# Two-stage attention and MoE kernel: who issues two early loads, who casts, and which pairs are transposed by TensorE

## The chip, the cores and the metric

One core of a Trainium2 chip. The metric is the device time of one execution, in microseconds (us). The kernel before takes 324.14 us, the median of 3 runs that lie between 324.01 and 324.51 us.

## The reference

What is computed, cut to its core (8 batches, 8 heads, 576 positions, head size 64; then 4608 tokens, 512 features, 2048 hidden):

```python
q_d, k_d, v_d = (mean over each 4 positions of q, k, v)
out_up    = repeat(softmax(q_d k_d^T / 8) v_d, 4)           # pooled attention
scores    = where(|i - j| < 4, q k^T / 8, -1e9)
out_local = softmax(scores) v                                # banded attention
x = (out_up + out_local) as [tokens, heads * head size]
h = x @ w_in
out = (h - tanh(h)) @ w_out
```

## The kernel before

**Pairs.** The attention works on pairs of heads, `p` = 0 to 31, four pairs (`j` = 0 to 3) to each batch `b`. What a pair makes is written, transposed, into `xT[j]`, 128 features by 576 tokens. The dense part takes a batch (512 tokens for an even one, 640 in pieces of 320 for an odd one): the first product L795 reads all four `xT[j]` of the batch, ScalarE takes tanh (L806), VectorE subtracts (L809, tile `gT`), and the second product L831 uses `gT` of the batch before; the result is copied (L846) and stored (L850).

**One pair, step by step.**
- Loads: q and k (`qkn`, L335) and v (`vst`, L368), all issued from SyncE's queue.
- Cast: `qkn` to bf16, reordered, in `qr`. Up to pair 15 these are two instructions at L521, one for each head of the pair, and each waits for both loads.
- Into feature-major form, tile `qk`: pairs 0 to 9 by nine TensorE transposes (L552) and a copy from PSUM (L556); pairs 10 to 31 by a DMA transpose (L526, tile `qT`) and two copies (L534). The list `TIN` says which.
- Pooling: `half` (L569) and `qkd` (L575 or L582).
- Scores: for pairs 0 to 3 a bias matrix is multiplied in first (L598, L607). Four of five blocks are s1 (L592), the fifth and the pooled scores are s2 (L592, L615). Up to pair 13 s1 and s2 stand apart in TensorE's order, from pair 14 they stand together (merged: the list `MERGE`, cut at `SPLIT`).
- Exponentials on ScalarE (L639 for s1, L652 and L655 for s2). A mask is multiplied in (L644, L660), or, from pair 12 on, a bias is added before the exponential (L634).
- Outputs: L669 (banded) and L675 (pooled) into PSUM; reciprocal and product on VectorE (L686, L688, tile `ln`).
- The way back: pairs 0 to 3 by twelve small products (L699, L702) and a copy (L767); pairs 4 to 7, 11 and 15 by TensorE transposes (L737, L738, L743), a copy of the pooled part (L762) and two adds (L754, L755); the rest by a DMA transpose (L705, tile `lT`) and two adds on GpSimd or VectorE (L717, L721). The list `XOUT` says which.
- v: a cast (L435, tile `vw`), pooled on TensorE (L449, L451, L471, L473) with a copy to `vd` (L454, L478) for the early pairs, by other means later.

**Order.** The instructions are first recorded as a list with costs and priorities; the class `Program` then simulates the engines, lets each pick what comes first by priority and dependence, picks an engine where a step has alternatives, and fixes the order on each engine's queue. So a change of a list or of a priority moves many instructions. The table `SHIFTS` adds to the priority of single steps, by their number, and can take an engine away from a step's choice. `P.shared` holds the steps that the planner takes to slow VectorE and GpSimd alike. Where the plan leaves TensorE idle before the dense part, filler matmuls (L1013) on a zeroed tile are put in; they use PSUM banks that are free.

**Limits on buffers around the change.** `qkn` has 4 buffers, `qr`, `qk`, `ln`, `lT`, `qT` and `E` have 2. From pair 12 on, the loads of a pair also wait in the plan until the DMA transpose L705 of the pair five before it has been issued (`GATE`, `BEHIND`).

Of the kernel before, what the change touches and what calls it, by code (L numbers as in the profile page):

```python
# [15 lines left out]
class Program:  # L16
# [21 lines left out]
    def op(self, eng, ns, fn, reads=(), writes=(), pri=0):  # L38
        i = len(self.ops)
        deps = set()  # L40
        for key in reads:
            if key in self.last_write:
                deps.add(self.last_write[key])
        for key in writes:
            if key in self.last_write:
                deps.add(self.last_write[key])
            deps.update(self.readers.get(key, ()))
        for key in reads:
            self.readers.setdefault(key, set()).add(i)
        for key in writes:  # L50
            self.last_write[key] = i
            self.readers[key] = set()
        deps.discard(i)
        if eng == "DMA":
            self.moves[i - 1] = i
        self.ops.append((eng, ns, fn, deps, pri))
        self.touch.append(set(reads) | set(writes))
        return i
# [93 lines left out]
    def emit(self, banks=None, end=None, filler=None):  # L152
        order = self.order()
        fill = {}
        if filler:
            until = min(self.start[i] for i in range(len(self.ops)) if end in self.touch[i])
            self.uses = {name: sorted(
                (self.start[i], self.start[i] + self.ops[i][1] + 200, i in self.fresh)
                for i in range(len(self.ops)) if self.touch[i] & set(keys))
                for name, keys in banks.items()}  # L160
            for i, name, room in self.idle(order, banks, until):
                if self.start[i] < 7000:
                    fill[i] = (name, int(min(8, room / 430) + max(0, 0.85 * room - 3440) / 220))
                else:
                    fill[i] = (name, int(0.8 * room / 220))
        for i in order:
            if i in fill:
                filler(*fill[i])
            if self.ops[i][2] is not None:
                self.ops[i][2]()  # L170
# [3 lines left out]
def kernel(  # L174
# [14 lines left out]
    NPAIR = B * NP  # L189
# [70 lines left out]
    P = Program()  # L260
# [66 lines left out]
    def load_qk(p):  # L327

        b, h0, s = p // NP, 2 * (p % NP), p % NQKN
        if LOAD[p] == 'row':  # L330
            for i, src in enumerate((q, k)):
                queue = nc.scalar if i and p < BYACT else nc.sync

# [151 lines left out]
    def attention(p):  # L485
# [16 lines left out]
        if LOAD[p] == 'tok':  # L502
            P.choice([(eng, ns, lambda fn=fn: fn(
                out=qr[s].rearrange("p a h d -> p (a h d)"),
                in_=qkn[sn].rearrange("p h c -> p (h c)"))) for eng, ns, fn in CAST_QK],
                     reads=[("qkn", sn, 0), ("qkn", sn, 1)],
                     writes=[("qr", s, 0), ("qr", s, 1)], pri=pri - 12)
            if TIN[p] == 'dma':
                op("SP", 1300, lambda: nc.sync.dma_start_transpose(
                    out=qk[s].rearrange("p i c -> p (i c)").rearrange(  # L510
                        "p (t c) -> p t c", c=128),
                    in_=qr[s].rearrange("p a h d -> p (a h d)")),
                   reads=[("qr", s, 0), ("qr", s, 1)],
                   writes=[("qk", s, 0), ("qk", s, 1), ("qTq", s)], pri=-50)
                op("DMA", 1300, None, reads=[("qTq", s), ("qr", s, 0), ("qr", s, 1)],
                   writes=[("qk", s, 0), ("qk", s, 1)], pri=pri)
        else:
            for hh in range(2):
                dst = qr[s][:, :, hh]
                srt = qkn[sn][:, hh].rearrange("p (a d) -> p a d", d=D)  # L520
                P.choice([(eng, ns, lambda dst=dst, srt=srt, fn=fn: fn(out=dst, in_=srt))  # L521
                          for eng, ns, fn in (any3[2:] if p >= CASTS else any3[:1] + any3[2:] if 0 < p < NOACT else any3)],
                         reads=[("qkn", sn, 0), ("qkn", sn, 1)],
                         writes=[("qr", s, hh)], pri=pri - 12)
        if TIN[p] == 'dma' and LOAD[p] == 'row':
            op("SP", 1300, lambda: nc.sync.dma_start_transpose(  # L526
# [5 lines left out]
            for i in range(2):  # L532
                def put(fn, i=i):
# [5 lines left out]
                         reads=[("qT", s)], writes=[("qk", s, i)], pri=pri)  # L539
        elif TIN[p] == 'pe':  # L540
            if p in APART:
# [153 lines left out]
        def back():  # L695
            for t, c, n in PIECES:
# [6 lines left out]
                         up[rows, t % 4, lead:lead + n], start=False, stop=True)  # L703
        if XOUT[p] == 'dma':
            op("SP", 1300, lambda: nc.sync.dma_start_transpose(  # L705
# [161 lines left out]


    EARLY, BIASED = 8, 4
    SPLIT = 14  # L870
    LOAD = ['row'] * NPAIR
    TIN = ['pe'] * 10 + ['dma'] * (NPAIR - 10)
    MERGE = [0] * EARLY + [2] * (SPLIT - EARLY) + [1] * (NPAIR - SPLIT)
    XOUT = ['pe' if p < 8 or p in (11, 15) else 'dma' for p in range(NPAIR)]
    PUT = [[("ACT", 535, A.copy), ("DVE", 620, V.tensor_copy)]] * 2
    W_PRI = [[5, 31, 32, 33], [-3, -2, -1, 0]]
    W_AT = (6, 6, 7, 7)
# [6 lines left out]
    V_ACT = ()  # L884
    FORE = 12
    GATE, BEHIND = range(12, NPAIR), 5
    BYACT = 0
    DIRECT, T_P = 16, 960
    T_IN, T_OUT = 1550, 1200
    NOACT = 0  # L890
# [1 line left out]
    HOLD = 2  # L892
    PADD = [p for p in range(NP, NPAIR) if XOUT[p] == 'pe']
    SOON = (0, 0, 0, 0)
# [68 lines left out]
    for p in range(2):  # L963
        prep_v(p)
    work = [attention(p) for p in range(NPAIR)]
    for a in work:
        next(a)
    next(work[0])
    for p in range(NPAIR):
# [23 lines left out]
    dense(B)  # L993

    SHIFTS = {
        70: (124, None), 80: (0, 'ACT'), 98: (211, None), 266: (212, None),
        325: (100, None), 388: (303, None), 643: (4864, None), 649: (0, 'DVE'),
        655: (50, None), 669: (50, None), 820: (62, None), 828: (-100, None),
        1248: (-105, None),
    }  # L1000
    for i, (shift, other) in SHIFTS.items():
        o = P.ops[i]
# [42 lines left out]
```

## Time and profile before

| | before |
|---|---|
| median of the runs | 324.14 us (324.01 to 324.51) |
| the profiled execution's own time | 324.28 us |
| its span, from the first to the last instruction | 322.5 us |
| TensorE matmul busy | 315.1 us, 98% of the span, 2661 instructions |
| VectorE, ScalarE, GpSimd busy | 216.5, 218.7, 194.1 us |
| granted TensorE clock, by the records | 1.00 |

The profile shows one execution. A line name such as L795 is a line of the kernel before; PE is TensorE's matmul, PEld its weight load, DVE VectorE, ACT ScalarE, POOL GpSimd, SP SyncE, which here only issues DMAs. In a timeline row stand the start in us, the length in us, the engine, line, operation, output and input, the shape, and how many instructions the row holds. Matmuls run into one another, so a row's length has some 0.15 us of a last matmul's tail in it: how long a stretch holds TensorE is read from one row's start to the next row's start. In brackets stand the idle time ahead of the row and what ended it.

### The profile page before, as it was taken

Reading aid. Unit: us, or ns where it says so; the run is one execution under the profiler, and the core shown is the slowest. Engines: PE = TensorE matmul, PEld = TensorE weight load, DVE = VectorE, ACT = ScalarE, POOL = GpSimd, SP = SyncE. Lnnn points to the kernel's source line nnn. Section 1 sums busy time; section 2 is a strip of 40 time slices with the busy share of each in tenths; the row PEclk is TensorE's granted clock in tenths of the full one; section 3 lists DMA queues with packets and bytes.
Section 4 is the critical chain, followed back from the end, with each engine's and each line's share of the span. In section 5 each row is a group of like instructions: output and inputs, shape, how many; then the busy total and the mean of one; then the engine's idle time right before and its main releaser. Section 6 shows DMA issues by size and latency. Waiting matters only on the chain.

```text
span 322.5 us, 7217 instructions
## 1 busy us (share of the span) xinstructions
PE 315.1 (98%) x2661; PEld 175.4 (54%) x2661; DVE 216.5 (67%) x397; ACT 218.7 (68%) x382; POOL 194.1 (60%) x271
## 2 busy tenths in 40 slices
PE   7889999999999999999999999999999999999996
PEld 3464545566654445666655445666654445566544
DVE  6778886887886577768667676766776454554312
ACT  2865997579997977699887769669975434555300
POOL 5578866468766789889999877997954100000000
PEclk9999999999999999999999999999999999999999
DMA  7999999699996899999999999998423211000012
GB/s 210 279 390 368 367 382 307 181 206 202 248 262 125 227 261 266 242 255 207 243 231 296 263 249 252 251 266 234 105 71 82 63 42 57 35 34 35 34 70 94
DMA packets 112832, 64.42 MB, mean 200 GB/s; under 512 B 90556, under 2 KB 96028, under 8 KB 112796
## 3 DMA queue, kind: packets, MB, share of 16 engines
q1 hardware_dynamic: 112796, 63.95, 77.4%
q8 instruction: 21, 0.34, 0.5%
q14 instruction: 15, 0.12, 0.1%
HBM read 42.96 MB, written 9.44 MB: 162 GB/s over the span
## 4 chain that ended last, share of the span: by engine, by line
PE 85%; DMA 6%; SPq 3%; POOL 2%; DVE 2%; issue 1%; ACT 0%; POOLq 0%
PE ps_hy L831 38%; PE ps_hy L795 36%; DMA gT<-in_moe_w_in_dram 3%; DMA qkn<-in_k_dram 3%; PE ps_ox L592 3%; PE ps_ox L669 3%; PE ps_ox L675 2%; SPq L335 2%; PE ps_ox L615 1%; SPq L368 1%; PE ps_ox L552 1%; DVE gT L809 1%; PE ps_ox L743 1%; POOL w_in_sb L428 1%; POOL E L660 1%
## 5 line engine op out<-in xcount | busy, mean ns | idle before, releaser
L795 PE MATMUL ps_hy<-xT,w_in_sb 128*128 128x320 bf16 (+1 forms) x768 | 147.9, 326 | 0.7 <-DVE gT L809 0.7
L831 PE MATMUL ps_hy<-w_out_sb,gT 128*128 128x512 bf16 (+2 forms) x608 | 144.4, 368 | 0.0
L809 DVE TENSOR_TENSOR gT<-ps_hy,u 128x320 bf16<-128x320 f32 (+1 forms) x192 | 103.4, 553 | 59.4 <-ACT u L806 57.5
L806 ACT ACTIVATE u<-ps_hy 128x320 f32<-128x320 f32 (+1 forms) x192 | 92.6, 496 | 55.8 <-PE ps_hy L795 50.2
L795 PEld LDWEIGHTS <-w_in_sb 128*128 128x128 bf16 x768 | 71.6, 98 | 52.4 <-issue 0.6
L831 PEld LDWEIGHTS <-gT 128*128 128x128 bf16 x608 | 56.5, 98 | 52.3
L569 POOL TENSOR_TENSOR half<-qk 128x576 f32<-128x576 bf16 x30 | 34.7, 1155 | 29.3 <-ACT qk L534 17.9
L534 ACT COPY qk<-qT 128x576 bf16<-128x576 bf16 x43 | 51.1, 1210 | 0.0
L688 DVE TENSOR_TENSOR ln<-ps_ox,r 128x896 bf16<-128x896 f32 x32 | 34.9, 1090 | 1.0
L521 POOL CAST qr<-qkn 128x576 bf16<-128x576 f32 x48 | 31.9, 677 | 4.6 <-DMA qkn<-in_k_dram 4.4
L639 ACT ACTIVATE E<-ps_ox 128x912 bf16<-128x912 f32 x28 | 26.2, 935 | 1.9 <-DVE ps_ox L634 1.2
L634 DVE TENSOR_TENSOR ps_ox<-ps_ox,bias 128x912 f32<-128x912 f32 x20 | 22.2, 1111 | 4.6 <-PE ps_ox L592 4.6
L846 DVE COPY y<-ps_hy 128x512 f32<-128x512 f32 (+2 forms) x22 | 14.1, 640 | 16.6 <-PE ps_hy L831 16.1
L435 POOL CAST vw<-vst 128x640 bf16<-128x640 f32 x31 | 23.6, 760 | 1.4 <-DMA vst<-in_v_dram 1.4
L660 POOL TENSOR_TENSOR E<-E,mask 128x240 bf16<-128x240 bf16 x23 | 15.2, 662 | 15.0 <-ACT E L652 14.7
L397 POOL TENSOR_TENSOR vp<-vp 72x512 f32<-72x512 f32 x16 | 20.3, 1268 | 0.0
L669 PEld LDWEIGHTS <-E 128*128 128x128 bf16 x320 | 16.3, 98 | 5.7
L669 PE MATMUL ps_ox<-vw,E 128*128 128x65 bf16 x320 | 19.4, 194 | 0.0
L655 ACT ACTIVATE E<-ps_ox 72x576 bf16<-72x576 f32 (+1 forms) x28 | 18.7, 668 | 0.0
L675 PE MATMUL ps_ox<-vd,E 128*128 128x65 bf16 (+1 forms) x256 | 18.2, 193 | 0.3 <-DVE vd L478 0.3
L592 PEld LDWEIGHTS <-qk 64*128 64x128 bf16 x320 | 9.1, 94 | 16.3 <-issue 12.5
L652 ACT ACTIVATE E<-ps_ox 128x240 bf16<-128x240 f32 x28 | 10.4, 370 | 7.4 <-PE ps_ox L615 6.2
(101 smaller groups left out, 264.6 us busy)
## 6 DMA issues: line engine op xcount, KB each, us to landing
vst<-in_v_dram SPq DMA_DIRECT2D x64, 160.0 KB, 4.3
qkn<-in_q_dram SPq DMA_DIRECT2D x32, 288.0 KB, 4.2
qkn<-in_k_dram SPq DMA_DIRECT2D x32, 288.0 KB, 4.3
out_dram<-y SPq DMA_DIRECT2D x35, 256.0 KB, 2.4
vp<-in_v_dram SPq DMA_DIRECT2D x15, 320.0 KB, 4.9
gT<-in_moe_w_in_dram SPq DMA_DIRECT2D x4, 1024.0 KB, 8.2
xT<-in_moe_w_out_dram SPq DMA_DIRECT2D x8, 256.0 KB, 4.6
gT<-in_moe_w_out_dram SPq DMA_DIRECT2D x2, 1024.0 KB, 8.7
```

Of the source, the lines that this page charges most:

```text
L435: P.choice([(eng, ns, lambda fn=fn: fn(out=vw[w][:, 2 * jj:2 * jj + 2, :, 0:64], in_=vst[s])) for eng, ns, fn in CAST_V[p >= NEARLY]], rea ...
L521: P.choice([(eng, ns, lambda dst=dst, srt=srt, fn=fn: fn(out=dst, in_=srt)) for eng, ns, fn in (any3[2:] if p >= CASTS else any3[:1] + any ...
L534: fn(out=full[:, i].rearrange("p (g a) -> p g a", a=A9), in_=qT[s][:, :, i::2].rearrange("p a g -> p g a"))
L569: eng.tensor_tensor(out=half, in0=four[:, :, :, 0:2], in1=four[:, :, :, 2:4], op=ALU.add)
L639: op("ACT", 820, lambda: A.activation(out=e1, in_=ps[:, :, 0:456], func=AF.Exp, scale=SCALE), reads=ts, writes=[("E", s, 0)], pri=pri)
L669: T.matmul(po[:, hh, 65 * t:65 * t + 65], E[s][:, c:c + 128], vw[w][:, 2 * jj + hh, t, :], start=True, stop=True)
L675: T.matmul(po[:, hh, o:o + 65], E[s][0:kp, c + gw * i:c + gw * i + 128], vd[w][0:kp, jj, 2 * hh + i, :] if direct else vd[w][:, i, 2 * jj ...
L688: op("DVE", 1010, lambda: V.tensor_tensor(out=ln[s].rearrange("p n (h d) -> p h n d", d=D), in0=blocks[:, :, :, 0:64], in1=r[s].unsqueeze( ...
L795: T.matmul(ps_hy[slot][:, 0:n], w_in_sb[:, dc, fc * 128:(fc + 1) * 128], xT[dc][:, t0 + c0:t0 + c0 + n], start=(dc == 0), stop=(dc == N_DC ...
L806: op("ACT", 90 + 76 * n // 100, lambda: A.activation(out=u[us][:, 0:n], in_=ps_hy[slot][:, 0:n], func=AF.Tanh), reads=[("hy", slot)], writ ...
L809: op("DVE", 70 + 105 * n // 100, lambda: V.tensor_tensor(out=gT[g][:, fc, c0:c0 + n], in0=ps_hy[slot][:, 0:n], in1=u[us][:, 0:n], op=ALU.s ...
L831: T.matmul(ps_hy[slot][:, 0:c1 - c0], gT[g][:, fc, ts * 128:ts * 128 + 128], w_out_sb[:, fc, c0:c1], start=(fc == 0), stop=(fc == N_FF - 1))
```

## The change

- The loads of k for pairs 0 and 1 are issued from ScalarE's queue (`BYACT` = 2).
- The casts L521 of q and k join the steps that the planner takes to be shared between VectorE and GpSimd, which makes it choose other engines.
- Pairs 10 and 11 come in through TensorE too (`TIN`), so in all pairs 0 to 11.
- Pairs 11 and 15 go back by DMA (`XOUT`), as their neighbours do.
- Merged scores from pair 12 on (`SPLIT`): pairs 12 and 13 are new in it.
- The number of fillers comes from another formula.
- The table of shifts is replaced as a whole, 22 entries for 13.

```diff
@@ Program.emit
-                if self.start[i] < 7000:
-                    fill[i] = (name, int(min(8, room / 430) + max(0, 0.85 * room - 3440) / 220))
-                else:
-                    fill[i] = (name, int(0.8 * room / 220))
+                slow = 430 if self.start[i] < 7000 else 220
+                fill[i] = (name, min(9, int(0.82 * room / slow)))
@@ the casts of q and k
+                P.shared.add(len(P.ops))
@@ the lists
-    SPLIT = 14
+    SPLIT = 12
-    TIN = ['pe'] * 10 + ['dma'] * (NPAIR - 10)
+    TIN = ['pe'] * 12 + ['dma'] * (NPAIR - 12)
-    XOUT = ['pe' if p < 8 or p in (11, 15) else 'dma' for p in range(NPAIR)]
+    XOUT = ['pe' if p < 8 else 'dma' for p in range(NPAIR)]
-    BYACT = 0
+    BYACT = 2
@@ the shifts, two of 13 and two of 22 entries
     SHIFTS = {
-        70: (124, None), 80: (0, 'ACT'),
...
+        73: (148, None), 75: (148, None),
...
```

The loads' queue is chosen by `queue = nc.scalar if i and p < BYACT else nc.sync` (L332, where `i` is 1 for k).

**What moves, place one: ScalarE at the start of the program.** Before, from the table load on (`qkn_72` and `qkn_73` hold q and k of pairs 0 and 1, `qr_87` is the cast for pair 0, `qr_88` for pair 1, `vd_84` the pooled v of pairs 0 and 1, `qk_89` is used by pairs 0 and 2, `qk_90` by pairs 1 and 3):

```order
L916 ACT_TABLE_LOAD
L916 CAST u_111<-lT_100 1x1
L556 COPY qk_89<-ps_ox 128x128x4
L521 CAST qr_88<-qkn_73 128x9x64
L639 ACTIVATE E_98<-ps_ts 128x912
L556 COPY qk_90<-ps_ox_118 128x128x4
L652 ACTIVATE E_98<-ps_ts 128x240
L655 ACTIVATE E_98<-ps_ts 128x640
L639 ACTIVATE E_99<-ps_ts_123 128x912
L556 COPY qk_89<-ps_ts 128x1152
L652 ACTIVATE E_99<-ps_ts_123 128x240
```

And in the changed kernel, whose line numbers are one or two lower:

```order
L333 DMA qkn_72<-in_k_dram 64x2x576
L333 DMA qkn_73<-in_k_dram 64x2x576
L915 ACT_TABLE_LOAD
L915 CAST u_111<-lT_100 1x1
L520 CAST qr_87<-qkn_72 128x9x64
L555 COPY qk_89<-ps_ox 128x128x4
L520 CAST qr_88<-qkn_73 128x9x64
L638 ACTIVATE E_98<-ps_ts 128x912
L555 COPY qk_90<-ps_ox_118 128x128x4
L651 ACTIVATE E_98<-ps_ts 128x240
L654 ACTIVATE E_98<-ps_ts 128x640
L638 ACTIVATE E_99<-ps_ts_123 128x912
```

Two DMA issues and a cast of pair 0 now stand ahead of the first copy. The next three rows behind these are `vd_84` (which VectorE made before), then L651 and L654 of pair 1, and only then the copy of pair 2, which before stood ahead of them, followed at once by the copy of pair 3.

**Place two: GpSimd, from its first cast on.** Before (`vst_76` to `vst_79` hold v of pairs 0 to 3):

```order
L521 CAST qr_87<-qkn_72 128x9x64
L521 CAST qr_88<-qkn_73 128x9x64
L435 CAST vw_81<-vst_76 128x10x64
L521 CAST qr_87<-qkn_74 128x9x64
L569 TENSOR_TENSOR half<-qk_90 128x576
L521 CAST qr_88<-qkn_75 128x9x64
L435 CAST vw_81<-vst_77 128x10x64
L435 CAST vw_82<-vst_79 128x10x64
L569 TENSOR_TENSOR half<-qk_90 128x576
L582 TENSOR_TENSOR qkd_97<-half 128x320
```

And in the changed kernel:

```order
L520 CAST qr_88<-qkn_73 128x9x64
L433 CAST vw_81<-vst_76 128x10x64
L520 CAST qr_87<-qkn_74 128x9x64
L433 CAST vw_81<-vst_77 128x10x64
L520 CAST qr_87<-qkn_74 128x9x64
L433 CAST vw_82<-vst_78 128x10x64
L433 CAST vw_82<-vst_79 128x10x64
L568 TENSOR_TENSOR half<-qk_89 128x576
L581 TENSOR_TENSOR qkd_96<-half 128x320
L568 TENSOR_TENSOR half<-qk_90 128x576
```

Pair 0's cast is gone from GpSimd, both of pair 2's are there, and pair 2's pooling stands behind the casts of v; pair 1's pooling and both casts of pair 3 went to VectorE. TensorE's order in this stretch moves as well: before, pair 2's transposes stand ahead of pair 1's s2; now the pooling of v (L471) and pair 1's s2 come first, and pair 2's transposes, pair 0's outputs, pair 3's transposes and pair 1's outputs follow.

**Place three: SyncE's queue around pair 11.** Before (`qT_91` in the first row is pair 12's DMA transpose in, `lT_100` pair 10's way back, `qkn_72` pair 16's load):

```order
L526 DMA_TRANSPOSE qT_91<-qr_87 128x9x128
L335 DMA qkn_74<-in_k_dram 64x2x576
L850 DMA out_dram<-y_114 128x512
L368 DMA vst_80<-in_v_dram 128x5x64 x2
L526 DMA_TRANSPOSE qT_92<-qr_88 128x9x128
L705 DMA_TRANSPOSE lT_100<-ln_106 128x7x128
L335 DMA qkn_75<-in_q_dram 64x2x576
L335 DMA qkn_75<-in_k_dram 64x2x576
L368 DMA vst_76<-in_v_dram 128x5x64 x2
L335 DMA qkn_72<-in_q_dram 64x2x576
```

And in the changed kernel, from pair 10's way back on:

```order
L704 DMA_TRANSPOSE lT_100<-ln_106 128x7x128
L333 DMA qkn_75<-in_q_dram 64x2x576
L333 DMA qkn_75<-in_k_dram 64x2x576
L366 DMA vst_76<-in_v_dram 128x5x64 x2
L525 DMA_TRANSPOSE qT_91<-qr_87 128x9x128
L849 DMA out_dram<-y_114 128x512
L704 DMA_TRANSPOSE lT_101<-ln_107 128x7x128
L333 DMA qkn_72<-in_q_dram 64x2x576
```

Pair 11's way back (`lT_101`) is a new row; it stands behind pair 14's transpose in and a store, and ahead of pair 16's loads. The transposes in of pairs 10 and 11, two rows that stood further up, are gone.

More of the change, by code (lines that the diff above doesn't have):

```diff
@@ L995 @@
     SHIFTS = {
[L996 to L999, printed above, removed]
+        73: (148, None), 75: (148, None), 98: (2058, None), 100: (750, 'ACT'),
[5 rows of a table added]
     }
```

5 rows, old and new, of the table SHIFTS are left out of this document.

## The prediction

> **What bounds the kernel now.** First the page's engine times, then a table by stages:
>
> ```profile
> PE 315.1 (98%) x2661; PEld 175.4 (54%) x2661; DVE 216.5 (67%) x397; ACT 218.7 (68%) x382; POOL 194.1 (60%) x271
> ```
> ```profile
> 0.00:7.00 7.00, 5.32 (x13) 1.69 (x14) 4.72 (x34) 1.47 (x2) 4.42 (x17) 1.00 0.65 191
> 7.00:24.00 17.00, 14.76 (x228) 9.75 (x229) 12.53 (x19) 12.64 (x19) 11.09 (x16) 1.00 1.02 334
> 24.00:62.00 38.00, 37.48 (x357) 19.58 (x353) 30.61 (x52) 27.96 (x49) 26.77 (x39) 1.00 0.98 326
> 62.00:120.00 58.00, 57.83 (x532) 32.31 (x529) 45.76 (x83) 49.85 (x89) 41.46 (x55) 1.00 0.94 219
> 120.00:250.00 130.00, 130.00 (x1129) 73.88 (x1128) 92.47 (x157) 101.58 (x175) 109.03 (x145) 1.00 0.98 220
> ```
>
> The columns are the stretch, its length, busy PE, PEld, DVE, ACT, POOL, the clock, the DMA share, GB/s. From 24 us on TensorE lacks 0.52 + 0.17 + 0.00 us in 226: there the time is TensorE's own work, and only work taken from it, or a new wait, counts. Before 24 us it is different: its busy time there holds fillers and tails, and a chain through the other engines sets when the dense work can start. So the change has two terms, TensorE's work behind 24 us and the length of the early chain.
>
> **Term one: TensorE's work.** Timeline rows of TensorE, in order: pair 4's transposes in, pair 11's way back, pair 13's scores in two pieces, pair 14's merged ones, each with the row behind it.
>
> ```profile
> 26.63 1.25 PE L795 MATMUL ps_hy<-xT,w_in_sb 128*128 128x512 bf16 x5
> 27.72 0.67 PE L552 MATMUL ps_ox<-ident,qr 128*128 128x128 bf16 x9
> 28.22 1.03 PE L795 MATMUL ps_hy<-xT,w_in_sb 128*128 128x512 bf16 x4
> ...
> 91.82 0.22 PE L737 MATMUL ps_ox<-ident,ln 128*128 128x128 bf16 x1
> 91.97 0.18 PE L738 MATMUL ps_ox<-ident,ln 32*128 32x32 bf16 x1
> 92.09 0.43 PE L743 MATMUL ps_ox<-ident,ln 120*128 120x120 bf16 x5
> 92.36 1.46 PE L831 MATMUL ps_hy<-w_out_sb,gT 128*128 128x512 bf16 x6
> ...
> 98.35 0.59 PE L831 MATMUL ps_hy<-w_out_sb,gT 128*128 128x512 bf16 x2
> 98.88 0.37 PE L592 MATMUL ps_ox<-qk 64*128 64x120 bf16 x8
> 99.19 1.47 PE L831 MATMUL ps_hy<-w_out_sb,gT 128*128 128x512 bf16 x6
> ...
> 103.32 0.23 PE L592 MATMUL ps_ox<-qk 64*128 64x120 bf16 x2
> 103.38 0.30 PE L615 MATMUL ps_ox<-qkd 64*128 64x160 bf16 x4
> 103.61 1.04 PE L795 MATMUL ps_hy<-xT,w_in_sb 128*128 128x512 bf16 x4
> ...
> 110.75 0.43 PE L592 MATMUL ps_ox<-qk 64*128 64x120 bf16 x10
> 111.02 0.30 PE L615 MATMUL ps_ox<-qkd 64*128 64x160 bf16 x4
> 111.25 0.60 PE L795 MATMUL ps_hy<-xT,w_in_sb 128*128 128x512 bf16 x2
> ```
>
> - A 512-wide matmul holds TensorE (27.72 − 26.63)/5 = 0.218 us. Nine transposes hold it 28.22 − 27.72 = 0.50. Pairs 10 and 11 add 2 × 0.50 = **+1.00**.
> - A way back holds it 92.36 − 91.82 = 0.54. Pairs 11 and 15 drop it: **−1.08**.
> - Pair 13's scores hold it 0.31 and 0.29 from start to start; ahead of the 0.31 stand 98.88 − 98.35 − 2 × 0.218 = 0.09 of a gap as the tile's rows go from 128 to 64. Merged, they hold it 0.50. I take 0.10 from the starts and 0.09 for the gap that goes: 0.19, for pairs 12 and 13 **−0.38** (−0.20 if the gap stays).
>
> Sum −0.46 (−0.28 to −0.46). What leaves and enters VectorE, ScalarE and GpSimd behind 24 us (two copies from `qT` become one from PSUM, adds become a DMA join) I cost at nothing, since TensorE lacks nothing from 120 to 250 us and 0.17 from 62 to 120; if that cover is gone, it shows as the waits priced below.
>
> **Term two: the early chain.** First, what held pair 0: the loads' issues, VectorE, TensorE.
>
> ```profile
> 1.60 0.61 SPq L335 DMA_DIRECT2D qkn<-in_k_dram  x1
> ...
> 2.90 0.61 SPq L335 DMA_DIRECT2D qkn<-in_k_dram  x1
> ```
> ```profile
> 5.40 0.77 DVE L319 TENSOR_SCALAR bias<-mask 128x576 bf16<-128x576 bf16 x1
> 6.09 0.74 DVE L521 CAST qr<-qkn 128x576 bf16<-128x576 f32 x1
> ```
> ```profile
> 5.35 0.67 POOL L521 CAST qr<-qkn 128x576 bf16<-128x576 f32 x1 [0.52 <-DMA qkn<-in_k_dram]
> ```
> ```profile
> 1.25 5.30 PE L1013 MATMUL ps_ts<-lT 128*128 128x512 bf16 x12 [1.25 <-DVE lT L915]
> 6.98 0.45 PE L552 MATMUL ps_ts<-ident,qr 128*128 128x128 bf16 x5 [0.43 <-DVE qr L521]
> ```
>
> GpSimd waited for k and began its cast at 5.35; VectorE made constants until 6.1 and only then cast the other half, with no wait for a load. TensorE's transposes came behind VectorE's cast, whose place in VectorE's order is the same in the changed kernel. So k by another queue brings pair 0 nothing, and ScalarE's cast of pair 0, ready by then, nothing either. The two issues gone from SyncE's queue (2 × 0.61 and the gaps, 1.3 us) let later loads go out earlier, but the DMA engines were busy 1.02 of the stretch from 7 to 24 us, so the loads land earlier by less: 0 to 1.3 us, I take 0.4, a third, as they already run full.
>
> [...]
>
> What shortens the chain is the new order. ScalarE's rows, before:
>
> ```profile
> 9.23 0.93 ACT L639 ACTIVATE E<-ps_ts 128x912 bf16<-128x912 f32 x1 [0.29 <-DVE half L569]
> ...
> 16.58 1.12 ACT L556 COPY qk<-ps_ts 128x1152 bf16<-128x1152 bf16 x1 [1.05 <-PE ps_ts L451]
> 17.95 0.93 ACT L639 ACTIVATE E<-ps_ts 128x912 bf16<-128x912 f32 x1 [0.25 <-PE ps_ox L669]
> 19.11 0.93 ACT L639 ACTIVATE E<-ps_ts 128x912 bf16<-128x912 f32 x1 [0.22 <-PE ps_ts L592]
> 20.85 0.37 ACT L652 ACTIVATE E<-ps_ts 128x240 bf16<-128x240 f32 x1 [0.81 <-PE ps_ts L615]
> ...
> 22.80 0.70 ACT L655 ACTIVATE E<-ps_ts 128x640 bf16<-128x640 f32 x1
> ```
> ```profile
> 23.41 0.32 PE L669 MATMUL ps_ox<-vw,E 128*128 128x65 bf16 x5
> ```
>
> From 9.23 on ScalarE runs from one early exponential to the next and stands for 1.05 + 0.25 + 0.22 + 0.81 = 2.3 us in this stretch. I laid the new order out by hand with these lengths. Pair 1's second exponential ends near 14.35, now behind the copy of pooled v; the copies of pairs 2 and 3 follow at once, to 16.5 (pair 3's before: 17.7); pair 2's exponential ends at 17.6. Pair 2's pooling on GpSimd, behind the casts of v, is ready near 18.2, so its s2 stands at 18.5; then a copy of pair 1's `xT`, new on ScalarE, and pair 3's exponential near 20.4. Pair 3's last exponential ends near 22.85 (23.50 before, the row at 22.80). TensorE's last early outputs follow it: pair 3's then begin near 22.8 against 23.41, the last row, and its way back and the dense work are earlier by as much. So **−0.6**, bounds 0 (the chain as long as before) and −1.5 (ScalarE loses two thirds of its 2.3 us).
>
> **New waits.** Pair 11 used to be added by VectorE right behind its products. Now its way is: reciprocal and product, issue, transfer, two adds on VectorE:
>
> ```profile
> L688 DVE TENSOR_TENSOR ln<-ps_ox,r 128x896 bf16<-128x896 f32 x32 | 34.9, 1090 | 1.0
> ```
> ```profile
> L717 DVE TENSOR_TENSOR xT<-lT x3: 398/441/527, 188.7 to 260.4; 128x240 bf16<-128x240 bf16 x3
> L721 DVE TENSOR_TENSOR xT<-lT x3: 502/965/1025, 189.2 to 260.7; 128x336 bf16<-128x336 bf16 x3
> ...
> DMA to landing us min/median/max: 2.9/3.9/6.0
> ```
>
> With some 0.3 for the reciprocal, 0.3 + 1.1 + 3.9 + 1.4 = 6.7 us from the pair's outputs (5.2 with the shortest of each row, 9.0 with the longest). TensorE's order has in between: 22 matmuls of 320 (0.136 each by width: 3.0), merged scores of pair 12 (0.5), 16 of 512 (3.5), pair 12's outputs (0.55): 7.6 us. The slack is 0.9, from +2.4 to −1.4. Behind VectorE's adds are queued the copy of y and pair 12's product, for which pair 12's own way back waits, not TensorE at once. On SyncE's queue pair 16's loads stand behind the new issue, five pairs ahead of their use. Pair 15 has some 13 us of such cover by the same count. I take **+0.1**, bounds 0 and 1.4.
>
> **Sum.** Against the profiled execution's 324.28 us (0.14 above the median 324.14): −0.46 − 0.6 + 0.1 = −0.96, so **323.3 us**, 0.26% under the median. A measurement of this kernel tells some 0.2%, that is 0.65 us, from no change: faster is under 323.5, slower over 324.8.
>
> **Rivals.**
> 1. **The early chain is no shorter.** Pair 2's pooling is on GpSimd behind four casts of v, the last of which waits for a load; before it was on VectorE. If that load or the copies come late by 0.6 us, the reordering gives nothing: 324.28 − 0.46 + 0.1 = 323.9, no change. For it: this chain is laid out by hand. Against it: ScalarE's 2.3 us of waits are there to be had.
> 2. **Cold start, ending slower.** Twelve fillers take 5.30 us, 0.44 each, twice the 0.218 of later; the first transposes start at 6.98 and five of them take 0.45 with the tail, so TensorE had become fast in between. The change leaves nine fillers: they end near 1.25 + 9 × 0.44 = 5.2, and TensorE then stands until 6.95. If it is fast only later, pair 0's nine transposes (+0.5), three fillers (+0.65) and the scores' 1872 columns (+0.8 by width) delay the first exponential, where ScalarE's chain begins, by up to 1.95; I take 1.6, with the rise inside the scores: 323.3 + 1.6 = 324.9. It decides when the rise falls behind pair 0's first transposes, and each transpose before the rise costs 0.056. For it: 3.9 us of activity for 5.3. Against: the rise in the trace could have come at any time after the last slow filler's start, and nine may do.
> 3. **Pair 11 arrives late** by 1.4 us: 323.3 − 0.1 + 1.4 = 324.6.
> 4. **More gain:** −1.5 in the early chain, no new wait: 322.3.
>
> [...]
>
> **Chances.** The forecast 0.42 (its own range 322.8 to 323.8), rival 1 0.17, rival 2 0.18, rival 3 0.10, rival 4 0.13. Faster takes three quarters of the forecast, a fifth of rival 1, and rival 4: 0.48. Slower takes two thirds of rival 2 and a third of rival 3, and 0.05 of the mishaps of rival 1 with a late pair 11: 0.20. The rest, 0.32, is no change. The range goes from 322.2 to 325.1: rival 4 and rival 2 with a little beyond each; outside lies what combines two of them.
>
> **What the new profile would show.** Right: pair 3's outputs begin near 22.8; pair 10's nine transposes and no L737 at pairs 11 and 15; one run of scores for pairs 12 and 13; TensorE's matmuls on `xT` after pair 12's outputs without a wait for pair 11's adds. Rival 1: pair 3's outputs at 23.4 again, with GpSimd's `qkd` of pair 2 after 18.5. Rival 2: pair 0's transposes twice as far apart as pair 4's and the first exponential after 9.5. Rival 3: idle ahead of the 512-wide L795, ended by L717 or L721. The prediction fails if new waits of TensorE behind 24 us sum to over 0.7 us at places I did not price.

## The result, and the profile after

The changed kernel takes 322.64 us (median of 20 runs, 321.22 to 326.13) against 324.38 us of the kernel before (20 runs, 323.69 to 331.1), a ratio of 0.9942 with a 95% interval of 0.9930 to 0.9953: 1.7 us or 0.58% faster; the ratio leaves out one slow run of each, 326.13 and 331.1. The forecast was 323.3, that is 0.98 under the profiled execution of before (324.28). The profiled execution of the change took 323.85 us with a span of 322.1, so it lies 1.2 above the median of its kernel, and this will matter.

The stretches of the table shown for before, now of the change (length, busy PE, PEld, DVE, ACT, POOL, clock, DMA share, GB/s):

```profile
0.00:7.00 7.00, 4.51 (x15) 1.71 (x16) 4.24 (x34) 2.14 (x3) 3.95 (x17) 1.00 0.71 221
7.00:24.00 17.00, 16.40 (x238) 10.14 (x238) 12.58 (x20) 12.87 (x20) 12.36 (x18) 1.00 1.05 348
24.00:62.00 38.00, 37.13 (x347) 20.13 (x352) 29.70 (x51) 28.92 (x52) 27.21 (x39) 1.00 1.01 329
...
120.00:250.00 130.00, 127.81 (x1089) 73.03 (x1105) 95.17 (x159) 97.85 (x169) 102.25 (x134) 1.00 0.98 211
```

TensorE's busy time can't be compared here: the trace holds 1089 matmuls and 1105 weight loads in the last stretch, so some matmul records are missing. The starts of rows do not suffer from that. I use three: the first transposes of pair 0, the first dense matmul, and the end of the last dense one. TensorE's rows of the change, beside 6.98, 23.41 and 23.98 before:

```profile
1.25 4.02 PE L1014 MATMUL ps_ts<-lT 128*128 128x512 bf16 x9 [1.25 <-DVE lT L914]
6.51 0.69 PE L551 MATMUL ps_ts<-ident,qr 128*128 128x128 bf16 x5 [1.24 <-DVE qr L520]
6.99 0.63 PE L551 MATMUL ps_ox<-ident,qr 128*128 128x128 bf16 x4
7.42 1.48 PE L1014 MATMUL ps_ts<-lT 128*128 128x512 bf16 x3
...
22.03 0.33 PE L668 MATMUL ps_ox<-vw,E 128*128 128x65 bf16 x5
...
22.63 0.59 PE L794 MATMUL ps_hy<-xT,w_in_sb 128*128 128x512 bf16 x2
```

Pair 0 starts 0.47 earlier, and pair 3's outputs 1.38 and the dense work **1.35 earlier** than before. That is so although pair 0 ran at half speed: five transposes take (6.99 − 6.51) = 0.48, 0.1 each, and three fillers 1.48 with a tail where three took 0.81 before. VectorE, GpSimd and ScalarE in that time:

```profile
5.39 0.31 DVE L317 TENSOR_SCALAR bias<-mask 128x576 bf16<-128x576 bf16 x1
5.62 0.75 DVE L520 CAST qr<-qkn 128x576 bf16<-128x576 f32 x1
```
```profile
6.79 0.66 POOL L520 CAST qr<-qkn 128x576 bf16<-128x576 f32 x1 [1.97 <-DMA qkn<-in_q_dram]
7.90 0.73 POOL L433 CAST vw<-vst 128x640 bf16<-128x640 f32 x1 [0.45 <-DMA vst<-in_v_dram]
```
```profile
10.04 0.93 ACT L638 ACTIVATE E<-ps_ts 128x912 bf16<-128x912 f32 x1 [1.12 <-PE ps_ts L591]
...
21.46 0.70 ACT L654 ACTIVATE E<-ps_ts 128x640 bf16<-128x640 f32 x1
```

The bias takes 0.31 in place of 0.77. GpSimd's cast of pair 1 waits for its load and stands at 6.79; before it stood at 7.73, also behind its load. ScalarE's first exponential is later by 0.81 (10.04 for 9.23), its last early one still earlier by 1.34 (21.46 for 22.80).

Around pair 12 TensorE's rows show the merged scores, pair 12's outputs and then the first 512-wide products, which need pair 11; VectorE's adds of pair 11 stand beside them:

```profile
89.15 0.43 PE L591 MATMUL ps_ox<-qk 64*128 64x120 bf16 x10
89.41 0.30 PE L614 MATMUL ps_ox<-qkd 64*128 64x160 bf16 x4
89.64 0.72 PE L794 MATMUL ps_hy<-xT,w_in_sb 128*128 128x320 bf16 x4
...
94.09 0.28 PE L674 MATMUL ps_ox<-vd,E 128*128 128x65 bf16 x4
94.21 2.75 PE L794 MATMUL ps_hy<-xT,w_in_sb 128*128 128x512 bf16 x12
```
```profile
92.84 0.41 DVE L716 TENSOR_TENSOR xT<-lT 128x240 bf16<-128x240 bf16 x1 [0.67 <-DMA lT<-ln]
93.17 1.03 DVE L720 TENSOR_TENSOR xT<-lT 128x336 bf16<-128x336 bf16 x1
...
158.05 1.57 DVE L720 TENSOR_TENSOR xT<-lT 128x336 bf16<-128x336 bf16 x1
...
192.23 0.89 DVE L716 TENSOR_TENSOR xT<-lT 128x240 bf16<-128x240 bf16 x1 [1.62 <-DMA lT<-ln]
```

Merged scores hold TensorE 0.49. Pair 11's adds waited 0.67 for the transfer, on VectorE, and were done at 94.2; TensorE went on at 94.21 with no gap. Later adds are slow (1.57) or wait (1.62). The whole bill of the two profiled executions: from the first dense matmul to the end of the last it is 319.71 − 23.98 = 295.73 before, and 319.07 − 22.63 = 296.44 now (last rows: 315.80 + 3.91 and 315.81 + 3.26). So in this execution the 1.35 at the start came through, the dense stretch grew by 0.7 where the forecast had 0.46 less of work and 0.1 more of waits, and the span fell by 0.4 only. Most executions of the change did better. The experiments say which of these numbers belong to the change.

### The profile page after: what moved, and what is told of

The parts are those of the page before. It is cut to its first block, busy times and chain, and to the rows that moved or that the text cites. A ratio compares the mean times of both kernels' runs of the same rounds, so it can differ in the third digit from the quotient of the medians.

```text
span 322.1 us, 7164 instructions
## 1 busy us (share of the span) xinstructions
PE 311.8 (97%) x2622; PEld 176.2 (55%) x2662; DVE 216.4 (67%) x399; ACT 218.9 (68%) x384; POOL 189.3 (59%) x263
## 4 chain that ended last, share of the span: by engine, by line
PE 79%; DMA 7%; DVE 5%; ACT 4%; issue 3%; SPq 1%; POOL 1%; ACTq 0%; DVEq 0%; POOLq 0%
PE ps_hy L794 33%; PE ps_hy L830 31%; PE ps_ox L591 3%; PE ps_ox L668 2%; DMA qT<-qr 2%; DMA lT<-ln 2%; DMA qkn<-in_k_dram 2%; PE ps_ox L674 2%; PE ps_ox L551 2%; DVE gT L808 1%; ACT u L805 1%; ACT qk L533 1%; PE ps_ox L614 1%; DVE xT L720 1%; ACT qk L555 1%
## 5 line engine op out<-in xcount | busy, mean ns | idle before, releaser
L794 PE MATMUL ps_hy<-xT,w_in_sb 128*128 128x320 bf16 (+1 forms) x760 | 146.0, 326 | 1.7 <-DVE gT L808 0.8
L830 PE MATMUL ps_hy<-w_out_sb,gT 128*128 128x512 bf16 (+2 forms) x577 | 139.3, 368 | 2.3 <-issue 1.1
L533 ACT COPY qk<-qT 128x576 bf16<-128x576 bf16 x40 | 47.6, 1200 | 4.4 <-DMA qT<-qr 4.4
L520 POOL CAST qr<-qkn 128x576 bf16<-128x576 f32 x44 | 29.5, 682 | 9.4 <-DMA qkn<-in_k_dram 3.4
L659 POOL TENSOR_TENSOR E<-E,mask 128x240 bf16<-128x240 bf16 x22 | 14.3, 650 | 8.8 <-ACT E L651 8.5
L654 ACT ACTIVATE E<-ps_ox 72x576 bf16<-72x576 f32 (+1 forms) x28 | 18.9, 676 | 0.0
L651 ACT ACTIVATE E<-ps_ox 128x240 bf16<-128x240 f32 x28 | 10.5, 374 | 6.8 <-PE ps_ox L614 6.7
```

The lines of the kernel that those rows point to most:

```text
L533: fn(out=full[:, i].rearrange("p (g a) -> p g a", a=A9), in_=qT[s][:, :, i::2].rearrange("p a g -> p g a"))
L794: T.matmul(ps_hy[slot][:, 0:n], w_in_sb[:, dc, fc * 128:(fc + 1) * 128], xT[dc][:, t0 + c0:t0 + c0 + n], start=(dc == 0), stop=(dc == N_DC ...
L830: T.matmul(ps_hy[slot][:, 0:c1 - c0], gT[g][:, fc, ts * 128:ts * 128 + 128], w_out_sb[:, fc, c0:c1], start=(fc == 0), stop=(fc == N_FF - 1))
```

## The experiments

Each kernel was timed in five rounds beside the kernel before, which gave 6 to 12 runs of each; the median of the kernel before lay between 324.12 and 324.35 in these rounds. Each ratio is to the kernel before in the same rounds. The table gives, of the one profiled execution of each: the start and spacing of pair 0's transposes, the start of GpSimd's cast of pair 1, the first dense matmul, the stretch to the end of the last dense matmul, and its time; then the median of all runs and the ratio to before.

| kernel | pair 0, spacing | pair 1's cast | first dense | stretch | this execution | median | ratio, 95% |
|---|---|---|---|---|---|---|---|
| before | 6.98, 0.056 | 7.73 | 23.98 | 295.73 | 324.28 | 324.38 | |
| the change | 6.51, 0.107 | 6.79 | 22.63 | 296.44 | 323.85 | 322.64 | 0.9942 (0.9930 to 0.9953) |
| 1 early part alone | 6.53, 0.055 | 6.66 | 21.53 | 298.96 | 325.38 | 325.81 | 1.0047 (1.0029 to 1.0065) |
| 2 late part alone | 6.90, 0.055 | 8.26 | 24.26 | 297.64 | 328.31 | 326.81 | 1.0080 (1.0056 to 1.0103) |
| 3 twelve fillers | 6.53, 0.055 | 8.34 | 22.41 | 296.76 | 325.37 | 323.43 | 0.9962 (0.9943 to 0.9982) |
| 4 k by SyncE | 6.53, 0.055 | 7.86 | 22.40 | 296.65 | 323.65 | 323.68 | 0.9982 (0.9970 to 0.9994) |
| 5 cast on GpSimd | 6.90, 0.055 | 6.72 | 22.97 | 295.24 | 322.87 | 322.63 | 0.9940 (0.9920 to 0.9961) |
| 6 no first fillers | 6.53, 0.106 | 6.90 | 22.99 | 297.84 | 325.46 | 323.46 | 0.9977 (0.9957 to 0.9998) |
| 7 four y | 6.51, 0.107 | 6.90 | 22.72 | 295.50 | 323.12 | 322.09 | 0.9932 (0.9917 to 0.9948) |
| 8 before, cast on ScalarE | 6.51, 0.107, from the seventh on 0.055 | 8.05 | 23.55 | 295.73 | 324.17 | 324.20 | 1.0007 (0.9996 to 1.0019) |
| 9 four y, twelve fillers | 6.51, 0.055 | 6.55 | 21.41 | 295.32 | 321.28 | 322.84 | 0.9952 (0.9932 to 0.9972) |
| 10 before, k by ScalarE | 6.88, 0.055 | 6.77 | 23.28 | 295.73 | 323.56 | 323.79 | 0.9986 (0.9976 to 0.9996) |
| 11 before, both | 6.51, 0.055 | 6.77 | 23.08 | 295.84 | 323.50 | 323.57 | 0.9982 (0.9970 to 0.9994) |
| 12 four y, adds on GpSimd | 6.53, 0.055 | 6.97 | 21.64 | 295.43 | 321.78 | 323.11 | 0.9969 (0.9948 to 0.9991) |

### The two parts alone (1 and 2)

The early part keeps the lists and the later shifts of before:

```diff
-    SPLIT = 12
-    TIN = ['pe'] * 12 + ['dma'] * (NPAIR - 12)
-    XOUT = ['pe' if p < 8 else 'dma' for p in range(NPAIR)]
+    SPLIT = 14
+    TIN = ['pe'] * 10 + ['dma'] * (NPAIR - 10)
+    XOUT = ['pe' if p < 8 or p in (11, 15) else 'dma' for p in range(NPAIR)]
     SHIFTS = {
...
-        669: (121, None), 674: (135, None), 815: (-111, None), 816: (-160, None),
-        1187: (-62, None), 1410: (-25, None),
+        643: (4864, None), 649: (0, 'DVE'),
+        655: (50, None), 669: (50, None), 820: (62, None), 828: (-100, None),
+        1248: (-105, None),
```

The late part is the reverse: the kernel before with the changed lists and the six later shifts.

> The change's early part alone (k of pairs 0 and 1 from ScalarE's queue, shared casts, new filler formula, the 16 shifts up to pair 9), with the lists and the later shifts of before. Theory A (most of the change's gain is the earlier start of the dense work, 1.4 us by pair 3's outputs at 22.03 against 23.41, of which later waits take a part back): about 323.2, that is 1.0 to 1.4 under before. Rival B (the middle is bound by the transfers as much as by TensorE, so an earlier start is given back whole): no change from before, within 0.4.

> The change's later part alone (pairs 10 and 11 in through TensorE, 11 and 15 back by DMA, merged scores from pair 12, the 6 later shifts), with the early order of before. Theory A: TensorE's work falls by 0.46, new waits take up to half of it back: 0.2 to 0.5 under before. Rival B (the later part carries the gain): 1.2 or more under before. Rival C (pair 11's way by DMA and the longer transfers cost more than the work saved): above before by 0.3 or more.

Both came out **slower** than before, by 0.47% and 0.80%. For the early part theory and rival both missed; for the late part the theory missed, and rival C had the sign, but the traces show another reason than the one it gave. The early part starts its dense work at 21.53, earlier than anything but one, and then loses 3.2 us in the dense stretch. TensorE's row and VectorE's, in the early part alone:

```profile
87.94 1.25 PE L794 MATMUL ps_hy<-xT,w_in_sb 128*128 128x320 bf16 x8 [1.67 <-DVE gT L808]
```
```profile
84.42 1.09 DVE L687 TENSOR_TENSOR ln<-ps_ox,r 128x896 bf16<-128x896 f32 x1
85.42 0.74 DVE L520 CAST qr<-qkn 128x576 bf16<-128x576 f32 x1
86.31 0.33 DVE L761 COPY pc<-ps_ox 128x160 f32<-128x160 f32 x1
86.67 0.41 DVE L753 TENSOR_TENSOR xT<-ps_ox,pc 128x240 bf16<-128x240 f32 x1
87.00 0.50 DVE L754 TENSOR_TENSOR xT<-ps_ox,pc 128x336 bf16<-128x336 f32 x1
87.41 0.89 DVE L808 TENSOR_TENSOR gT<-ps_hy,u 128x320 bf16<-128x320 f32 x2
```

Five other instructions, 3 us, stand in one piece on VectorE ahead of the subtraction that frees TensorE's bank. The late part alone has the like at 88.3 to 90.9, with a wait of 1.52, and at its end the last copy waits 2.54 for a store. The planner makes the order of all engines anew for every list, and the shifts that mend an order are meant for one order alone. So what the halves cost says nothing of what each edit is worth, and from here on I changed kernels without a new plan: the order of all instructions stays, and one engine, one queue or one count is changed as the instructions are written out.

### What holds pair 0: the cast (5 and 8)

```diff
-                P.choice([(eng, ns, lambda dst=dst, srt=srt, fn=fn: fn(out=dst, in_=srt))
+                P.choice([(eng, ns, lambda dst=dst, srt=srt, fn=GP.tensor_copy if eng == "ACT" and p == 0 else fn: fn(out=dst, in_=srt))
```

Kernel 8 is the kernel before with the reverse (`A.copy` for "POOL").

> The changed kernel with pair 0's second cast on GpSimd, where it stood before, in place of ScalarE. Theory (GpSimd's cast slowed VectorE's bias from 0.31 to 0.77 us, and so held pair 0's other cast by 0.47): the bias takes 0.7 to 0.8 again, VectorE's cast of pair 0 begins at about 6.1 in place of 5.62, and the median rises by 0.3 to 0.5. Rival (the bias was long by chance or by what it read): it stays at 0.31 and the time does not change.

> The kernel before with pair 0's second cast on ScalarE in place of GpSimd, nothing else moved. Theory (GpSimd's cast beside VectorE's constants slows these by 0.4): bias takes 0.31 and VectorE's cast begins at 5.6 in place of 6.1, pair 0's transposes at 6.5, and the median falls by 0.2 to 0.5. Rival (pair 0's start has slack in before's order): rows as said, but the dense work starts where it did, and the time does not change.

The rows came as the theory said in both directions: with the cast on GpSimd VectorE's cast began at 6.01 and pair 0 at 6.90, with the cast on ScalarE at 5.6 and 6.51. What GpSimd slowed was another constant, though, in kernel 5 the last copy of `up` (0.59 for 0.22) and not the bias, since GpSimd's cast came a little earlier there (4.98 for 5.35). In before's order the dense work began 0.43 earlier for it. The medians do not show it: 322.63 and 322.64, 324.20 and 324.24 beside it. So the step is real in the early chain, and whether a run is shorter for it **stays open** at this resolution.

### What the queue is worth (4, 10 and 11)

```diff
-                def issue(i=i, src=src, queue=queue):
-                    queue.dma_start(
+                def issue(i=i, src=src):
+                    nc.sync.dma_start(
```

Kernel 10 is the kernel before with the two issues on ScalarE ahead of its table load, and kernel 11 has the cast of kernel 8 besides.

> The changed kernel with k of pairs 0 and 1 issued from SyncE's queue again, in the order q, k, q, k; nothing else moved. Theory (the queue is worth little: VectorE's constants hold pair 0): VectorE's first cast begins at 5.6 as in the change, and the median stays within 0.3 of the change's 322.64. Rival (the queue is what made the early part earlier): pair 0's cast waits for k, which landed at 5.2 before, pair 3's outputs begin 0.4 or more later than the change's 22.03, and the median rises by 0.5 or more.

> The kernel before with k of pairs 0 and 1 issued from ScalarE's queue, ahead of its table load, nothing else moved. Theory (the queue brings all later early loads forward by 1.1, and so the early chain): GpSimd's cast of pair 1 at 6.7 in place of 7.73, and dense work from 23.2 to 23.5 in place of 23.98; the median falls by 0.4 to 0.8. Rival (in before's order the chain hangs on pair 0 and ScalarE): the casts move, the dense work does not, and the time stays within 0.2.

> The kernel before with k of pairs 0 and 1 from ScalarE's queue and pair 0's second cast on ScalarE, nothing else moved: the two edits that the change names first, without its order. Theory (each takes off its own part): pair 0's transposes at 6.5, pair 1's cast at 6.7, dense work from 22.8 to 23.1; the median falls by 0.8 to 1.2. Rival (the change's early gain is from its order of TensorE and ScalarE): dense work from 23.5 or later, and the median falls by less than 0.4.

Here my theory was wrong in kernel 4 and the rival right on the time: with k back on SyncE's queue the median is 323.68, **1.0 above the change**. Not by pair 0, as the rival had it, which starts at 6.53 as in the change, but by all that follows. SyncE's queue reaches the first loads of v 1.1 earlier without the two issues of k; its row before, and in the change:

```profile
3.55 1.16 SPq L368 DMA_DIRECT2D vst<-in_v_dram  x2
...
2.48 1.20 SPq L366 DMA_DIRECT2D vst<-in_v_dram  x2
```

In kernel 4 the row is at 3.56 again. GpSimd's rows with k by SyncE:

```profile
7.86 0.66 POOL L520 CAST qr<-qkn 128x576 bf16<-128x576 f32 x1 [3.02 <-DMA qkn<-in_k_dram]
9.01 0.73 POOL L433 CAST vw<-vst 128x640 bf16<-128x640 f32 x1 [0.48 <-DMA vst<-in_v_dram]
10.75 0.67 POOL L520 CAST qr<-qkn 128x576 bf16<-128x576 f32 x1 [1.02 <-DMA qkn<-in_k_dram]
11.88 0.73 POOL L433 CAST vw<-vst 128x640 bf16<-128x640 f32 x1 [0.46 <-DMA vst<-in_v_dram]
```

Each of them waits for a load, and each stands 1.1 to 1.4 later than in the change (6.79, 7.90, 9.38, 10.48). The dense work at 22.40 seems no later than the change's 22.63; but kernel 4's pair 0 ran at full speed, and beside the other starts at full speed (21.41 to 21.64, below) it is 0.8 to 1.0 late. In before's order the queue alone brings pair 1's cast from 7.73 to 6.77 and the dense work from 23.98 to 23.28; the median falls by 0.14% (0.04 to 0.24), and with the cast too, to 23.08 and by 0.18% (0.06 to 0.30). That is in the theory's direction and short of its 0.8 to 1.2 for both: 324.22 − 323.57 = 0.65. What is between 23.08 and the 21.4 to 21.6 of the changed order is the **order's own part, 1.5**, with the choice of engines that goes with it.

### The clock at the start (3, 6 and 9)

```diff
                 fill[i] = (name, min(9, int(0.82 * room / slow)))
+                if fill[i][1] == 9:
+                    fill[i] = (name, 12)
```

With 0 in place of 12 for kernel 6; kernel 9 has the four buffers of kernel 7 besides.

> The changed kernel with twelve fillers ahead of pair 0's transposes in place of nine, nothing else moved. Theory (the profiled run of the change ran pair 0's transposes, fillers and first scores at half speed, and the runs from 321.2 to 324.0 differ by when the clock rose): the transposes stand 0.056 apart, the runs lie closer together, and the median falls by 0.3 to 0.8 against the change's 322.64. Rival (the spread is from the transfers): no difference, same spread.

> The changed kernel without the fillers ahead of pair 0's transposes, so that TensorE starts them cold in every run. Theory (a cold start delays the first exponential to about 10.0 from 8.8, and the dense work by 0.7): the transposes stand 0.1 apart, the first exponential begins at 10.0 or later, and the median is 0.3 to 1.0 above the change's 322.64. Rival (the start of the early chain has slack): pair 3's outputs begin where they did and the median stays.

> The changed kernel with four buffers for y and twelve fillers ahead of pair 0. Theory (a start in which the clock is up by pair 0 has the dense work begin 1.1 earlier, 21.53 against 22.63, and the late q of pair 1 in the first run with twelve fillers was chance): pair 0's transposes 0.056 apart, GpSimd's cast of pair 1 at 6.7 to 6.9, the first dense matmul at 21.5 to 21.7, and a median of 321.4 to 321.9, the fastest here. Rival (twelve fillers do something to the loads): pair 1's cast after 8 again, dense work from 22.4, and 323 or more.

The early part of the program (up to about 60 us) is the same in the change, in the early part alone and in kernels 3, 6, 7, 9 and 12 but for fillers. Where pair 0's transposes stand 0.055 apart and the loads are in time the dense work begins at 21.41 to 21.64 (kernels 1, 9, 12); where they stand 0.107 apart, at 22.63 to 22.99 (the change, 6, 7). So a cold start costs **some 1.1 at the dense work** (from 0.99 to 1.58 between single executions). The loads are not behind this: pair 1's cast is as late in kernel 12 (6.97) as in the three that start cold (6.79 to 6.90). Nine fillers left it cold in the change and in kernel 7, and not in kernels 1, 4 and 12. In kernel 5 pair 0's transposes were fast (0.055 apart) and the next three fillers slow (0.41 each), and the record of the granted clock shows it for once (0.58, then 0.78):

```profile
7.00:10.00 3.00, 3.00 (x22) 1.28 (x21) 2.12 (x3) 1.26 (x2) 1.80 (x3) 0.58 1.15 363
10.00:12.00 2.00, 2.00 (x22) 1.48 (x21) 0.94 (x2) 1.71 (x3) 1.55 (x3) 0.78 1.14 339
```

From 3.50 to 7.00 that record is 1.00. If it is 1.00 again behind the slow stretch, 0.58 puts the fall to half speed near 7.48 and 0.78 the rise near 10.88: my estimate, from these two rows alone. The rows of TensorE agree: pair 1's transposes stand 0.10 apart from 10.02 on. What sets that stretch, and why the same nine fillers have two outcomes, no run here shows.

Without first fillers the median is 323.46, 0.8 above the change, as the theory said, though the cold start is not the whole of it: the profiled execution of kernel 6 also lost 2.6 in the dense stretch (297.84 for 295.24). Twelve fillers should then have been better than nine, and they were **not**: 323.43 and 322.84, against 322.64 and 322.09 with nine. In the profiled execution of kernel 3 the clock was up, but pair 1's q landed late (its cast at 8.34), dense work began at 22.41, and at the end the last copy waited for a store:

```profile
320.85 0.29 DVE L847 COPY y<-ps_hy 128x128 f32<-128x128 f32 x1 [2.24 <-DMA out_dram<-y]
```

Kernel 9's profiled execution has the early start (21.41) and is the shortest of the profiled ones, 321.28, but its other runs go up to 323.9. So the clock explains a part of the difference from run to run. Another part is not the clock, as kernel 3's profiled execution shows; which part the other runs had was not seen.

### The end and the adds (7 and 12)

```diff
-    y = fixed("y", [128, Dm], FP32, 3)
+    y = fixed("y", [128, Dm], FP32, 4)
...
-            ys = yn[0] % 3
+            ys, y4 = yn[0] % 3, yn[0] % 4
```

and `y[y4]` for `y[ys]` in the copy and the store. Kernel 12 has besides:

```diff
-            P.choice([("DVE", 880, lambda: join(V))][:p in JOIN_V] +
+            P.choice([("DVE", 880, lambda: join(GP if p > 15 else V))][:p in JOIN_V] +
```

> The changed kernel with four buffers for the result rows y in place of three, the order of all instructions as it was. Theory (where a run is 1 to 2 us above the others, the last copy has waited for a store of y to land before it could write its buffer, as it did for 2.24 us in the run with twelve fillers): the last copy never waits for a store, the runs lie closer together and the median falls by 0.2 to 0.8 under the change's 322.64. Rival (the end of the span is set by the last stores' landing anyway): no change.

> The changed kernel with four buffers for y, and with the adds of pairs 18, 19, 23, 30 and 31 behind their DMA on GpSimd in place of VectorE, at the place that the order gave them. Theory (the change put four more of these adds on VectorE, 7 for 3, where they stand slowed beside GpSimd or wait for the transfer, and the subtractions behind them make TensorE wait 0.6 to 1.1 at 155 to 160 and 193 in some executions): no wait of TensorE for L808 there, the runs closer together, and a median 0.2 to 0.6 under the 322.09 of the kernel with four buffers alone. Rival (on GpSimd the adds come later, and TensorE waits for the xT itself): TensorE waits for L716 or L720 near 160 and 195, and the median rises.

Four buffers gave the lowest median, 322.09, ratio 0.9932 (0.9917 to 0.9948); its interval overlaps that of the change and it has six runs, so whether it is better is not settled. The wait that it was to remove was in none of the profiled executions of the change and of kernels 5, 7, 9 and 12, where the last copy waits for TensorE. With the adds on GpSimd the waits of TensorE at 155 to 160 and 193 are gone, and the stretch is 295.43, as the theory said. TensorE's waits in that execution, whole (us in total, times, longest):

```profile
PE ps_ts L551 <- DVE qr L520: 1.6, 1, 1.6
PE ps_ts L1014 <- DVE lT L914: 1.3, 1, 1.3
PE ps_hy L830 <- issue: 1.1, 7, 0.2
PE ps_ox L469 <- POOL vw L433: 0.6, 1, 0.6
PE ps_hy L794 <- issue: 0.5, 3, 0.2
PE ps_hy L794 <- DVE gT L808: 0.2, 1, 0.2
```

("issue" is where matmul records are missing.) But kernels 5, 7 and 9 were without those waits too, with the adds on VectorE, and the median rose to 323.11. So the theory's median **missed**; what makes the other runs of kernel 12 longer was not seen.

## Why the prediction was right, and where it was not

- **The sign held; the work of TensorE (−0.46) is not shown as a whole.** The dense stretch is 295.73 to 295.84 in the four kernels with before's lists and order. In those with the changed lists and order it is 295.24, 295.32, 295.43 and 295.50 in kernels 5, 9, 12 and 7, which lack the late waits of the change: 0.23 to 0.49 less than 295.73. But a stretch holds waits too, and before has three for `gT` in it, kernel 9 one. Before's rows, then kernel 9's:

```profile
30.43 1.89 PE L795 MATMUL ps_hy<-xT,w_in_sb 128*128 128x512 bf16 x8 [0.22 <-DVE gT L809]
44.47 1.02 PE L795 MATMUL ps_hy<-xT,w_in_sb 128*128 128x512 bf16 x4 [0.26 <-DVE gT L809]
83.79 1.79 PE L795 MATMUL ps_hy<-xT,w_in_sb 128*128 128x320 bf16 x12 [0.17 <-DVE gT L809]
...
27.83 1.46 PE L796 MATMUL ps_hy<-xT,w_in_sb 128*128 128x512 bf16 x6 [0.22 <-DVE gT L810]
```

  Without these waits 295.73 − 0.65 = 295.08 stand against 295.32 − 0.22 = 295.10. So the shorter stretch can be the waits alone. Of the term's parts, merged scores took 0.49 for the forecast 0.50, but the transposes of pairs 10 and 11 took 0.60 and 0.59 for 0.50. They have scores on 64 rows behind them, where the forecast's row had a 128-row product; in the change:

```profile
67.90 0.67 PE L551 MATMUL ps_ox<-ident,qr 128*128 128x128 bf16 x9
68.50 0.23 PE L591 MATMUL ps_ox<-qk 64*128 64x120 bf16 x2
```

- **The early chain (−0.6): this term was mis-sized, and it is the step that failed.** It measured −1.35 with the cold start of the profiled execution, and −2.3 to −2.6 in kernels 1, 9 and 12, where the clock was up. Three things went wrong in it. First, "k by another queue brings pair 0 nothing" was right for pair 0, but the other loads were given 0.4, "as they already run full", and then not counted in the sum at all. Measured, GpSimd's casts of pairs 1 and 2 came 0.94 to 0.96 earlier than before, in the change and in kernel 10, dense work 0.70 (kernel 10), the median 0.4 to 1.0 (kernels 10 and 4). I had read the DMA share of 7 to 24 us, where it is 1.02; but these loads are issued from 0.8 us on, and up to 3.5 us the engines had room:

```profile
0.00:3.50 3.50, 2.25 (x6) 0.88 (x7) 1.53 (x23) 1.47 (x2) 2.56 (x13) 1.00 0.33 88
3.50:7.00 3.50, 3.07 (x9) 0.81 (x8) 3.19 (x11) 0.00 (x0) 1.86 (x5) 1.00 0.96 293
```

  (the kernel before; in the change the second row moves 359 GB/s at a share of 1.11). What k by ScalarE's queue gave here is the time of its two issues on SyncE's, 0.61 each: the first loads of v went out 1.07 earlier (2.48 for 3.55). Second, ScalarE's cast of pair 0 was to bring nothing, since VectorE's constants hold pair 0; but the cast on GpSimd was what made one of these constants long, and pair 0 came 0.47 earlier. Third, the order itself: −0.6 by hand, 1.5 between kernels 11 and 9, 12 and 1.
- **Rival 2, the cold start: it happened**, in the profiled execution among others, and delayed the first exponential to 10.04, from 8.76 in kernel 9. At the dense work it cost some 1.1 for the 1.6 said, and did not make the kernel slower than before, since the rest of the early chain gained more than that.
- **Rival 3, pair 11 late: did not happen.** Its adds waited 0.33 to 1.66 in eight executions with the changed order, and TensorE not for them. Pair 15, the other pair that newly goes back by DMA, was given 13 us of cover, and that was too much in one of the eight: in kernel 6 TensorE waits for its add.

```profile
133.07 1.38 PE L796 MATMUL ps_hy<-xT,w_in_sb 128*128 128x320 bf16 x9 [0.51 <-DVE xT L722]
```

- **New waits (+0.1): too small for the profiled execution, at places that I did not price.** With 295.24 as the stretch without them, it has 1.2: adds of pairs 18, 19 and 23, which the plan moved to VectorE (7 such adds for 3), and a late transpose in at 211. The prediction named over 0.7 of such waits as its own sign of failure, and by it that execution is one; kernels 5, 9 and 12 have no such waits.
- **Rival 1, no shorter chain: did not happen.** Rival 4, more gain in the early chain and no new wait, gave 322.3, which is nearer to the measured 322.64 than 323.3 is.
- **How near 323.3 came is in part luck.** The measured 322.64 lies in the whole range but not in the forecast's own, 322.8 to 323.8. And it is that near only because errors of opposite sign met: the chain was worth 2.3 to 2.6 and not 0.6, and a cold start that the sum had left out took some 1.1 of it back in a part of the runs, late waits 1.2 in the profiled one.

With these sizes and no late waits a run of the change comes out as most were measured: 22.63 + 295.24, 2.9 to the end of the span and 1.8 around it are 322.6 with a cold start, and 321.4 with 21.5. The runs of the change have seven of 20 between 321.2 and 321.9, nine between 322.5 and 322.9. That the two groups are the two starts is argued from the sums; no run shows both its start and its place but the profiled ones. Kernels 3 and 9 speak against so simple an account: in all seven traces with twelve first fillers the clock was up by the seventh of pair 0's nine transposes, and yet only three of these two kernels' 20 runs are under 322.

## What to carry to other kernels

Price a transfer that is moved to another queue in the stretch where it is issued, not where the DMA engines are fullest: at this kernel's start they had room (a share of 0.33 up to 3.5 us), and the queue's 0.61 us for each issue was what the later loads waited for. Ask of an engine that holds the chain not only what it does there but what runs beside it: here VectorE's bias took 0.77 beside GpSimd's cast and 0.31 without it. And where a planner makes the order, undo an edit only as the instructions are written out: a half of this change under a new plan was slower than none of it.

## What the runs showed of the hardware that was not expected

Some of VectorE's constants and adds took two to three times as long beside GpSimd: the bias 0.31 alone and 0.77 beside a cast, a copy of `up` 0.22 and 0.59. The change has seven adds of each line on VectorE. L716 took 0.40 alone and 0.40 to 0.89 beside GpSimd; L720 took 0.49 to 0.50 in the three with nothing of GpSimd's beside them and 0.96 to 1.57 in the four others. The longest of them in the change ran beside this row of GpSimd's, and ended 0.37 after it:

```profile
157.82 1.43 POOL L395 TENSOR_TENSOR vp<-vp 72x512 f32<-72x512 f32 x1
```

Why VectorE is slower there no run here shows. And the record of the granted clock read 1.00 in the change's first 10 us, while transposes stood 0.107 apart in place of 0.056: the spacing of equal instructions told the half speed, the record did not.
